# Attention and two expert layers on one core: the wide layer's sums kept in PSUM, and one ring of eight SBUF tiles for its streamed blocks

## The chip, the cores and the metric

The kernel runs on one core of a Trainium2 chip. The metric is device time in microseconds (us) of one execution; a comparison takes the median of several executions. The engines are called as the profile calls them: PE is TensorE's matmul, PEld its weight load, DVE is VectorE, ACT is ScalarE, POOL is GpSimd, and SP issues the DMAs.

## What is computed

```python
def reference(**kwargs):
    ...
    attn_out = _attn_ref(**attn_kwargs)               # (2, 8, 768, 64), masked by hash buckets
    B, H, S, D = attn_out.shape
    x = np.ascontiguousarray(attn_out.transpose(0, 2, 1, 3)).reshape(B * S, H * D)
    x = _moe_ref(x=x, **moe_kwargs)                   # h = max(x @ w_in, 0); (h * h) @ w_out
    return _moe2_ref(x=x, **moe2_kwargs)

def _moe2_ref(x, w_in, w_out, alpha) -> np.ndarray:
    h = x @ w_in                                      # 1536 x 512 by 512 x 2048
    g = np.maximum(h, 0.0) + alpha * np.minimum(h, 0.0)
    return (g @ w_out).astype(np.float32)             # 1536 x 2048 by 2048 x 512
```

There are 1536 tokens, 512 model columns and 2048 hidden columns in both layers. The change touches the second layer only, `_moe2_ref`.

## The kernel before

**Layout of the time.** Attention runs first, then layer one in four chunks of 384 tokens (`feed_forward`), with the rest of attention and the preparation of layer two's weights beside it. Layer two follows in two token halves n = 0 and 1. Each half is a hidden stage, `wide_hidden(n)`, and then a project stage, `whole_project(n)`. The order on the clock of the trace is: hidden 1 (571.2 to 646.2 us), project 1 (to 732.4), hidden 2 (to 811.3), project 2 (last sums at 896, then the output leaves).

**Precision.** Every float32 product is split into a rounded high part and the rest (low), each a float32r tile, and a product takes three matmuls: high by high, high by low, low by high. So every weight or value that PE reads has first gone through an ACT copy (the high part) and a subtract on POOL or DVE (the low part).

**Hidden stage.** The product x @ w_in is done by Strassen and Winograd's scheme: seven products of half-size blocks in place of eight, with sums of blocks before and after. The sums of weights were made earlier and lie in DRAM (`ws`); the sums of x are made by `x_sums`. The stage has 8 iterations f. In each, `w_load(f + 2)` (L888) starts a DMA of 896 KB into `wraw`, a tile of the pool `slots` (3 tiles of 2048 float32 per partition). `w_part(f + 1)` splits it into `wp`: two ACT copies (L895, 128x1024 and 128x768) and two POOL subtracts (L896), into a tile of the pool `parts` (2 tiles). Then 42 matmuls of 128x384 on PE (L873, L874, L875: six for each of the seven products) go into four PSUM banks a, b, c, d in the order 0(a), 4(b), 3(c), 1(a), 5(d), 6(c), 2(d). PSUM has 8 banks for this, so two iterations fit.

Between the products DVE adds blocks (`add`, L879): u2 = b + p1, u4 = c + u2, and the sums h = d + u4, c + u2 and d + u2. p1 is an ACT copy of bank a (L929). Product 1 overwrites a after p1 has read it, product 6 goes on in c after u4 has read it, and product 2 overwrites d after the sum d + u4 has read it. Each of the four results then takes the leaky step, `leaky`: up = Relu(h) on ACT (L910), down = Relu(-h) on ACT (L911), and g = down * (-alpha) + up as a scalar_tensor_tensor on DVE (L912). For quarter 11 the ACT steps read PSUM and write the SBUF tiles `up` and `down`; for the other three, h is the SBUF tile that `add` wrote, and L911 writes over it. So L912 always reads two SBUF tiles. g stays in SBUF for the project stage.

**Project stage.** For each of 16 steps f, `part(f)` brings in one block of w_out by DMA (`wp`, L954, 256 KB), splits it by an ACT copy (L955) and a DVE subtract (L956), and splits the block of g by an ACT copy of 128x768 (`gp`, L959) and a POOL subtract (L960). `wp` and `gp` are each one tile of the pool `slots`. Then 18 matmuls of 128x512 follow, over six banks: 12 with g's high part (L969, L970) and 6 with its low part (L975; in the last step L972, bank by bank). `part(f + 2)` is written after step f. In project 1, `second_x` and `x_sums` for the other half run beside.

**What sets the order.** The Tile scheduler places the instructions of each engine by a priority and by when a tile becomes free; a tile of a pool is handed out once its earlier reader is done. The order on each engine is fixed when the program is built, so a waiting instruction holds all that stand behind it on its engine. SP's DMA queue works in the same way.

Of the kernel before, what the change touches and what calls it, by code (L numbers as in the profile page):

```python
# [7 lines left out]
F32 = mybir.dt.float32  # L8
F32R = mybir.dt.float32r
# [3 lines left out]
AF = mybir.ActivationFunctionType  # L13
ALU = mybir.AluOpType
# [15 lines left out]
def kernel(  # L30
# [20 lines left out]
    nc = tc.nc  # L51
# [3 lines left out]
    P = 128  # L55
    T = S // 2
# [8 lines left out]
    scale = 1.0 / float(D) ** 0.5  # L65

    def pool(name, bufs, stack=ctx, **kw):
        return stack.enter_context(tc.tile_pool(name=name, bufs=bufs, **kw))
# [13 lines left out]
    state = {"attention": True, "moe": False, "s": 0, "m": 0, "h": 0, "whole": state_whole}  # L82
# [35 lines left out]
    def f32(ap):  # L118
        return ap.bitcast(F32)
# [489 lines left out]
    HM = DM // 2  # L609
# [26 lines left out]
    PLACE = (0, 1, 4, 2, 3, 5, 6)  # L636
# [157 lines left out]
    KH = KDM // 2  # L794
# [70 lines left out]
    def slot(name, dt=F32R):  # L865
        return state["slots"].tile([P, 2048], dt, tag="slot", name=name)

    def bank():
        return state["ps"].tile([P, 512], F32, tag="b", name="b")

    def products(ps, w, m, gh, gl, first, last):
        ms = slice(m * P, (m + 1) * P)
        nc.tensor.matmul(ps, w[:, 0, ms], gh, start=first, stop=False, skip_group_check=True)  # L873
        nc.tensor.matmul(ps, w[:, 0, ms], gl, start=False, stop=False, skip_group_check=True)  # L874
        nc.tensor.matmul(ps, w[:, 1, ms], gh, start=False, stop=last, skip_group_check=True)  # L875

    def add(name, ps, x, pool=None):
        t = (pool or state["sums"]).tile([P, T], F32, tag=name, name=name)
        nc.vector.tensor_tensor(t, ps, x, ALU.add)  # L879
        return t  # L880
# [4 lines left out]
    def w_load(f):  # L885
        if f < NF:
            raw_sums[f] = slot("wraw", F32)[:, 0:7 * HM].rearrange("p (a n) -> p a n", n=HM)
            nc.sync.dma_start(out=raw_sums[f], in_=w_sum[f])  # L888

    def w_part(f):  # L890
        if f < NF:
            w = raw_sums.pop(f)
            t = state["parts"].tile([P, 2, 7, HM], F32R, tag="wp", name="wp")
            for i, j in ((0, 4), (4, 7)):
                nc.scalar.activation(t[:, 0, i:j], w[:, i:j], AF.Copy)  # L895
                nc.gpsimd.tensor_tensor(t[:, 1, i:j], w[:, i:j], f32(t[:, 0, i:j]), ALU.subtract)  # L896
            loaded[f] = t

    def wide_hidden(n, between):


        xh, xl = x_parts[n]
        half = [state["g"].tile([P, NF, 2, T], F32, tag=f"g{i}", name=f"g{i}") for i in range(2)]
        quarter = {f"{i + 1}{k + 1}": half[i][:, :, k] for i in range(2) for k in range(2)}
        def leaky(q, h, f):

            col = f + NF * (q[0] == "2")
            up = state["sums"].tile([P, T], F32, tag="up", name="up")
            down = h if q != "11" else state["sums"].tile([P, T], F32, tag="h", name="down")
            nc.scalar.activation(up, h, AF.Relu)  # L910
            nc.scalar.activation(down, h, AF.Relu, scale=-1.0)  # L911
            nc.vector.scalar_tensor_tensor(  # L912
                quarter[q][:, f], down, neg_alpha[:, col:col + 1], up, ALU.mult, ALU.add
            )

        for f in range(NF):
            w_load(f + 2)
            w_part(f + 1)
            w = loaded.pop(f)

            def product(p, ps, first):
                for kk in range(KH):

                    products(ps, w[:, :, PLACE[p]], kk, xh[:, p, kk], xl[:, p, kk], first and kk == 0, kk == KH - 1)

            a, b, c, d = [bank()[:, 0:T] for _ in range(4)]
            product(0, a, True)
            p1 = state["sums"].tile([P, T], F32, tag="p1", name="p1")
            nc.scalar.activation(p1, a, AF.Copy)  # L929
            product(4, b, True)  # L930
            u2 = add("u2", b, p1)
            product(3, c, True)
            u4 = add("u4", c, u2)
            product(1, a, False)
            leaky("11", a, f)
            product(5, d, True)
            leaky("22", add("h", d, u4), f)
            product(6, c, False)
            leaky("12", add("h", c, u2), f)
            product(2, d, False)  # L940
            leaky("21", add("h", d, u2), f)
            between(f)
        return half, quarter

# [85 lines left out]
    state["xraw"] = pool("xraw", 3)  # L1030
    state["xt"] = pool("xt", 2)
    state["xc"] = pool("xc", 1)
    state["slots"] = pool("slot", 3)
    state["parts"] = pool("parts", 2)
    neg_alpha = const.tile([P, KFF], F32, name="neg_alpha")
    nc.vector.tensor_scalar(neg_alpha, alpha_sb[:, 0:KFF], -1.0, None, ALU.mult)
    turned = Background(
# [3 lines left out]
    w_load(0)  # L1041
    w_load(1)
    w_part(0)
    layer1.close()
    state["ps"] = pool("ps2", 8, space=PSUM)
    state["g"] = pool("g", 1, side="right")
    state["sums"] = pool("sums", 2, side="right")
    state["out"] = pool("out", 2, side="right")

    half, quarter = wide_hidden(0, lambda f: None)  # L1050
    steps = second_x(2, bank) + x_sums(1)

# [5 lines left out]
    w_load(0)  # L1058
    w_load(1)
    w_part(0)  # L1060
    half, quarter = wide_hidden(1, lambda f: None)
    whole_project(1, half, lambda f: None)

# [64 lines left out]
```

## Time and profile before

| What | Value |
|---|---|
| Time, three executions | 899.75, 905.48, 909.24 us (median 905.48) |
| The profiled execution | 905.19 us, of which the span is 903.3 us |
| Mean granted clock of TensorE | 0.985 |
| PE busy | 795.3 us (88% of the span) |
| DVE busy | 569.8 us (63%) |
| ACT busy | 510.8 us (57%) |
| POOL busy | 352.6 us (39%) |
| DMA | 143.86 MB, 159 GB/s on average |

The span is the time from the first to the last instruction of the trace; 1.9 us of the execution lie around it. Busy times are those of instructions that do work, and a matmul's own time overlaps with the next one's, so PE's share says little of how much faster it could go. The rows further down are read by stage.

### The profile page before, as it was taken

The page shows a single profiled execution, that of the slowest core. Times are in us where ns is not written, and L with a number is a line of the kernel's source. Part 1 is how long each engine was busy: PE and PEld are TensorE (multiplying, and loading weights), DVE is VectorE, ACT ScalarE, POOL GpSimd, SP SyncE. Part 2 cuts the span into 40 slices and gives each one's busy share as a digit, 9 for nine tenths or more (in the row PEclk, how much of TensorE's full clock was granted, in tenths as well). Part 3 has the DMA queues.
Part 4 walks back from the last instruction along what each step waited for, and adds up shares of the span by engine and source line. Part 5 has one row for each costly group of instructions (what it writes and reads, how often), then busy time and mean ns, then how long its engine had stood idle before and what let it go on. Part 6 is the DMA issues. An engine that isn't in the chain of part 4 may idle for free.

```text
span 903.3 us, 12522 instructions
## 1 busy us (share of the span) xinstructions
PE 795.3 (88%) x4324; PEld 638.1 (71%) x4324; DVE 569.8 (63%) x847; ACT 510.8 (57%) x988; POOL 352.6 (39%) x257
## 2 busy tenths in 40 slices
PE   4899899999999999899999999888978888798885
PEld 2565777777677677677776999777756677786664
DVE  6678799887676577887886352488671138871111
ACT  4677687876565465565656676456542246552222
POOL 1002223334366366433325756235233355423332
PEclk9999899999999999999999999999999999999999
DMA  4957688887867866777566854030011173101112
GB/s 125 227 147 230 202 265 256 250 239 199 247 204 228 204 218 235 249 249 240 190 209 200 290 169 129 15 108 12 24 48 46 51 241 122 54 12 46 48 53 87
DMA packets 56879, 143.86 MB, mean 159 GB/s; under 512 B 7440, under 2 KB 11824, under 8 KB 56816
## 3 DMA queue, kind: packets, MB, share of 16 engines
q1 hardware_dynamic: 56816, 143.07, 51.2%
q8 instruction: 34, 0.56, 0.3%
q14 instruction: 29, 0.24, 0.1%
HBM read 96.82 MB, written 25.48 MB: 135 GB/s over the span
## 4 chain that ended last, share of the span: by engine, by line
PE 20%; DVE 13%; issue 12%; POOL 6%; ACT 6%; DMA 5%; SPq 1%; POOLq 0%; DVEq 0%; ACTq 0%
DVE g L912 4%; POOL gp L960 3%; PE b L969 2%; PE b L970 2%; PE b L975 2%; DMA wf<-w 2%; PE m L424 2%; POOL wp L896 2%; PE b L873 1%; ACT gp L959 1%; DVE u L879 1%; ACT wp L895 1%; PE b L875 1%; PE b L874 1%; PE h L681 1%
## 5 line engine op out<-in xcount | busy, mean ns | idle before, releaser
L644 POOL TENSOR_TENSOR wl<-wf,wh 128x512 fp32r<-128x512 f32 x80 | 111.1, 1391 | 114.0 <-ACT wh L643 86.3
L694 POOL TENSOR_TENSOR gl<-g,gh 128x384 fp32r<-128x384 f32 x64 | 72.9, 1139 | 112.4 <-ACT g L691 53.1
L960 POOL TENSOR_TENSOR gp<-g,gp 128x768 fp32r<-128x768 f32 x32 | 59.4, 1856 | 133.9 <-ACT gp L959 133.9
L643 ACT ACTIVATE wh<-wf 128x512 fp32r<-128x512 f32 x128 | 79.6, 627 | 55.3 <-PE h L682 28.0
L969 PE MATMUL b<-wp,gp 128*128 128x512 f32 x192 | 78.4, 408 | 28.2 <-ACT gp L959 28.2
L393 ACT ACTIVATE sm<-s,low 128x768 f32<-128x768 f32 x84 | 75.5, 898 | 49.1 <-DVE low L390 48.8
L873 PE MATMUL b<-xph,wp 128*128 128x384 f32 x224 | 78.8, 355 | 25.5 <-DVE u L879 23.4
L390 DVE TENSOR_REDUCE low<-s 128x1 f32<-128x768 f32 x84 | 79.9, 952 | 29.7 <-PE s L385 29.0
L896 POOL TENSOR_TENSOR wp<-wraw,wp 128x1024 fp32r<-128x1024 f32 (+1 forms) x32 | 71.7, 2261 | 68.6 <-ACT wp L895 58.2
L956 DVE TENSOR_TENSOR wp<-wp 128x512 fp32r<-128x512 f32 x32 | 22.1, 690 | 114.7 <-ACT wp L955 114.7
L385 PE MATMUL s<-k,q 128*128 128x384 f32 x336 | 81.3, 361 | 13.3 <-ACT sm L393 11.9
L408 PE MATMUL m<-ident,sm 128*128 128x128 f32 x531 | 85.8, 277 | 4.3 <-ACT q L318 1.4
L408 PEld LDWEIGHTS m<-ident,sm 128*128 128x128 f32 x531 | 65.7, 141 | 21.9 <-ACT q L318 2.2
L681 PE MATMUL h<-xh,wh 128*128 128x384 f32 x212 | 78.9, 372 | 2.4 <-ACT xh L452 1.6
L385 PEld LDWEIGHTS s<-k,q 128*128 128x128 f32 x336 | 59.1, 194 | 30.6 <-ACT sm L393 20.4
L875 PE MATMUL b<-xph,wp 128*128 128x384 f32 x224 | 75.4, 344 | 2.2 <-POOL wp L896 2.2
L874 PE MATMUL b<-xpl,wp 128*128 128x384 f32 x224 | 76.9, 343 | 0.0
L912 DVE SCALAR_TENSOR_TENSOR g<-h,neg_alpha,up 128x384 f32<-128x384 f32 x48 | 69.0, 1458 | 11.3 <-ACT h L911 11.3
L970 PE MATMUL b<-wp,gp 128*128 128x512 f32 x192 | 75.3, 392 | 0.0
L683 PE MATMUL h<-xh,wl 128*128 128x384 f32 x212 | 72.5, 342 | 0.8 <-DMA w<-we 0.8
L682 PE MATMUL h<-xl,wh 128*128 128x384 f32 x212 | 72.5, 342 | 0.6 <-POOL xl L453 0.6
L969 PEld LDWEIGHTS b<-wp,gp 128*128 128x128 f32 x192 | 36.0, 188 | 47.2 <-ACT gp L959 40.5
(176 smaller groups left out, 1865.5 us busy)
## 6 DMA issues: line engine op xcount, KB each, us to landing
wf<-w SPq DMA_DIRECT2D x96, 256.0 KB, 2.9
wbits<-in_w_in_dram SPq DMA_DIRECT2D x32, 512.0 KB, 4.8
wbits<-in_w_out_dram SPq DMA_DIRECT2D x32, 512.0 KB, 4.2
wraw<-ws SPq DMA_DIRECT2D x16, 896.0 KB, 4.9
q<-q SPq DMA_DIRECT2D x48, 192.0 KB, 3.0
w<-wf SPq DMA_DIRECT2D x32, 256.0 KB, 2.6
wp<-w SPq DMA_DIRECT2D x32, 256.0 KB, 2.6
k<-kh SPq DMA_DIRECT2D x14, 384.0 KB, 5.9
```

The lines of the kernel that those rows point to most:

```text
L385: nc.tensor.matmul(ps[:, a, 0:HALF], self.q[:, h, i, qs], self.k[:, h, i, ks], start=i == 0, stop=i == 1)
L408: nc.tensor.transpose(ps[:, i * P:(i + 1) * P], pp[:, b * P:(b + 1) * P], ident)
L644: engine.tensor_tensor(lo, w, f32(hi), ALU.subtract)
L681: nc.tensor.matmul(hp, wih[:, ks], xh[:, kk, :], start=first, stop=False)
L873: nc.tensor.matmul(ps, w[:, 0, ms], gh, start=first, stop=False, skip_group_check=True)
L874: nc.tensor.matmul(ps, w[:, 0, ms], gl, start=False, stop=False, skip_group_check=True)
L875: nc.tensor.matmul(ps, w[:, 1, ms], gh, start=False, stop=last, skip_group_check=True)
L896: nc.gpsimd.tensor_tensor(t[:, 1, i:j], w[:, i:j], f32(t[:, 0, i:j]), ALU.subtract)
L912: nc.vector.scalar_tensor_tensor(quarter[q][:, f], down, neg_alpha[:, col:col + 1], up, ALU.mult, ALU.add)
L960: nc.gpsimd.tensor_tensor(t[:, 1], x, f32(t[:, 0]), ALU.subtract)
L969: nc.tensor.matmul(a, g[:, 0, b], w[:, 0], start=f == 0, stop=False)
L970: nc.tensor.matmul(a, g[:, 0, b], w[:, 1], start=False, stop=False)
```

## The change

In `leaky` the second ACT step writes over its input in every case, and in three of four sums of the hidden stage a new helper, `onto`, takes the place of `add`: it writes the sum in PSUM, over the bank that it read, or, for quarter 22, into bank b, which u2 has read by then. So h is always a PSUM bank, L912 reads one PSUM bank and one SBUF tile, and the tiles `h` and `down` are gone. A bank is held until L912 has read it.

The pool `parts` is gone and `slots` grows from 3 tiles to 8. `w_part` takes two of these tiles, one for the high and one for the low part.

```diff
@@ products
-        nc.tensor.matmul(ps, w[:, 0, ms], gh, start=first, stop=False, skip_group_check=True)
+        nc.tensor.matmul(ps, w[0][:, ms], gh, start=first, stop=False, skip_group_check=True)
...
@@ w_part
-            t = state["parts"].tile([P, 2, 7, HM], F32R, tag="wp", name="wp")
+            t = [slot("wp")[:, 0:7 * HM].rearrange("p (a n) -> p a n", n=HM) for _ in range(2)]
             for i, j in ((0, 4), (4, 7)):
-                nc.scalar.activation(t[:, 0, i:j], w[:, i:j], AF.Copy)
-                nc.gpsimd.tensor_tensor(t[:, 1, i:j], w[:, i:j], f32(t[:, 0, i:j]), ALU.subtract)
+                nc.scalar.activation(t[0][:, i:j], w[:, i:j], AF.Copy)
+                nc.gpsimd.tensor_tensor(t[1][:, i:j], w[:, i:j], f32(t[0][:, i:j]), ALU.subtract)
@@ wide_hidden
             up = state["sums"].tile([P, T], F32, tag="up", name="up")
-            down = h if q != "11" else state["sums"].tile([P, T], F32, tag="h", name="down")
             nc.scalar.activation(up, h, AF.Relu)
-            nc.scalar.activation(down, h, AF.Relu, scale=-1.0)
+            nc.scalar.activation(h, h, AF.Relu, scale=-1.0)
             nc.vector.scalar_tensor_tensor(
-                quarter[q][:, f], down, neg_alpha[:, col:col + 1], up, ALU.mult, ALU.add
+                quarter[q][:, f], h, neg_alpha[:, col:col + 1], up, ALU.mult, ALU.add
             )
+
+        def onto(ps, x, to=None):
+
+            to = ps if to is None else to
+            nc.vector.tensor_tensor(to, ps, x, ALU.add)
+            return to
...
-            leaky("22", add("h", d, u4), f)
+            leaky("22", onto(d, u4, b), f)
             product(6, c, False)
-            leaky("12", add("h", c, u2), f)
+            leaky("12", onto(c, u2), f)
             product(2, d, False)
-            leaky("21", add("h", d, u2), f)
+            leaky("21", onto(d, u2), f)
...
-    state["slots"] = pool("slot", 3)
-    state["parts"] = pool("parts", 2)
+    state["slots"] = pool("slot", 8)
```

In the changed kernel the lines behind `leaky` stand 6 further down (`part` is at L960 to L966 there, `onto` adds at L919, and p1 is L935). The scheduler places some instructions anew. First DVE, in the second iteration of hidden 1, from u2 on; the numbers are those of tiles and banks. Before:

```order
L879 TENSOR_TENSOR u2_6710<-b_6693,p1_6702 128x384
L879 TENSOR_TENSOR u4_6718<-b_6694,u2_6710 128x384
L879 TENSOR_TENSOR h_6737<-b_6695,u4_6718 128x384
L912 SCALAR_TENSOR_TENSOR g0_6601<-down_6727,neg_alpha_5790,up_6726 128x384
L879 TENSOR_TENSOR h_6749<-b_6694,u2_6710 128x384
L912 SCALAR_TENSOR_TENSOR g1_6602<-h_6737,neg_alpha_5790,up_6739 128x384
L879 TENSOR_TENSOR h_6761<-b_6695,u2_6710 128x384
L912 SCALAR_TENSOR_TENSOR g0_6601<-h_6749,neg_alpha_5790,up_6751 128x384
L912 SCALAR_TENSOR_TENSOR g1_6602<-h_6761,neg_alpha_5790,up_6763 128x384
```

And DVE in the same iteration of the changed kernel:

```order
L879 TENSOR_TENSOR u2_6706<-b_6689,p1_6698 128x384
L879 TENSOR_TENSOR u4_6714<-b_6690,u2_6706 128x384
L912 SCALAR_TENSOR_TENSOR g0_6599<-b_6688,neg_alpha_5787,up_6722 128x384
L919 TENSOR_TENSOR b_6689<-b_6691,u4_6714 128x384
L919 TENSOR_TENSOR b_6690<-b_6690,u2_6706 128x384
L912 SCALAR_TENSOR_TENSOR g1_6600<-b_6689,neg_alpha_5787,up_6733 128x384
L919 TENSOR_TENSOR b_6691<-b_6691,u2_6706 128x384
L912 SCALAR_TENSOR_TENSOR g0_6599<-b_6690,neg_alpha_5787,up_6744 128x384
L912 SCALAR_TENSOR_TENSOR g1_6600<-b_6691,neg_alpha_5787,up_6755 128x384
```

There are nine instructions in both; the leaky step of quarter 11 now stands ahead of the sum for quarter 22, the sum that product 2 waits for.

The second place is ACT, from the last iterations of hidden 1 to the start of project 1. Before, from the last leaky steps on:

```order
L910 ACTIVATE up_7246<-h_7244 128x384
L911 ACTIVATE h_7244<-h_7244 128x384
L959 ACTIVATE gp_7267<-g0_6601 128x768
L816 ACTIVATE xraw_7297<-b_7323 128x4x128
L816 ACTIVATE xraw_7297<-b_7354 128x4x128
L955 ACTIVATE wp_7288<-wp_7288 128x512
L959 ACTIVATE gp_7292<-g0_6601 128x768
```

And after, in the last iteration and behind it:

```order
L965 ACTIVATE gp_7293<-g0_6599 128x768
L910 ACTIVATE up_7219<-b_7155 128x384
L911 ACTIVATE b_7155<-b_7155 128x384
L832 ACTIVATE xph_7389<-xraw_6563 128x768
L961 ACTIVATE wp_7289<-wp_7289 128x512
L965 ACTIVATE gp_7324<-g0_6599 128x768
L961 ACTIVATE wp_7320<-wp_7320 128x512
L965 ACTIVATE gp_7355<-g0_6599 128x768
```

Before, gp_7267 is the block of step 1, and it stands behind the last leaky step; in the changed kernel gp_7293 is that of step 3, and it stands ahead of it.

The third place is POOL in layer one's last chunk, where wl is the low part of one of layer one's weights, gl that of its hidden values, and wp that of layer two's. Before:

```order
L694 TENSOR_TENSOR gl_5849<-g_5847,gh_5848 128x384
L896 TENSOR_TENSOR wp_6605<-wraw_6573,wp_6605 128x768
L644 TENSOR_TENSOR wl1_5880<-wf_5823,wh1_5879 128x512
L694 TENSOR_TENSOR gl_5899<-g_5897,gh_5898 128x384
L644 TENSOR_TENSOR wl1_5931<-wf_5856,wh1_5930 128x512
L694 TENSOR_TENSOR gl_5950<-g_5948,gh_5949 128x384
L644 TENSOR_TENSOR wl1_5982<-wf_5906,wh1_5981 128x512
L694 TENSOR_TENSOR gl_6007<-g_6005,gh_6006 128x384
```

And after:

```order
L694 TENSOR_TENSOR gl_5896<-g_5894,gh_5895 128x384
L896 TENSOR_TENSOR wp_6604<-wraw_6570,wp_6603 128x1024
L644 TENSOR_TENSOR wl1_5928<-wf_5853,wh1_5927 128x512
L896 TENSOR_TENSOR wp_6604<-wraw_6570,wp_6603 128x768
L694 TENSOR_TENSOR gl_5947<-g_5945,gh_5946 128x384
L644 TENSOR_TENSOR wl1_5979<-wf_5903,wh1_5978 128x512
L896 TENSOR_TENSOR wp_6683<-wraw_6601,wp_6682 128x1024
L896 TENSOR_TENSOR wp_6683<-wraw_6601,wp_6682 128x768
L694 TENSOR_TENSOR gl_6004<-g_6002,gh_6003 128x384
```

In the changed kernel the split of a third block of layer two (wp_6683) has moved up into layer one, between two of its own subtracts; before, it stood behind the last of them.

## Rows read from the trace of the kernel before

**Rows 1.** The page's costliest groups: L912 (busy us, mean ns | idle before, releaser).

```profile
L912 DVE SCALAR_TENSOR_TENSOR g<-h,neg_alpha,up 128x384 f32<-128x384 f32 x48 | 69.0, 1458 | 11.3 <-ACT h L911 11.3
```

**Rows 2.** Windows by stage: us, then busy per engine (instructions), PEclk, DMA share, GB/s.

```profile
500.00:540.00 40.00, 40.00 (x241) 39.81 (x241) 15.44 (x15) 30.15 (x57) 25.30 (x20) 1.00 0.66 228
571.20:646.20 75.00, 62.51 (x337) 59.63 (x338) 59.26 (x71) 42.89 (x84) 28.90 (x13) 0.98 0.14 44
646.20:732.40 86.20, 71.25 (x301) 54.12 (x300) 26.58 (x30) 32.06 (x46) 28.52 (x16) 1.00 0.19 59
732.40:811.30 78.90, 64.80 (x338) 60.97 (x337) 60.20 (x73) 45.67 (x89) 37.19 (x17) 0.96 0.31 103
811.30:893.10 81.80, 67.11 (x277) 50.40 (x276) 11.98 (x18) 23.40 (x33) 27.58 (x15) 1.00 0.16 45
```

**Rows 3.** PE's waits by line, in 571:646, 646:732.4, 732.4:808 and 808:904 (total, times, longest us).

```profile
PE b L873 <- DVE u L879: 12.5, 6, 2.1
...
PE b L969 <- ACT gp L959: 14.2, 14, 2.5
...
PE b L873 <- DVE u L879: 10.9, 6, 2.1
PE b L875 <- POOL wp L896: 2.2, 2, 1.4
...
PE b L969 <- ACT gp L959: 14.0, 15, 0.9
PE b L972 <- POOL gp L960: 0.7, 1, 0.7
```

**Rows 4.** The chain that ended last, 571:735: start us, us, what.

```profile
590.32 1.60 DVE g L912
...
592.70 2.18 DVE g L912
...
677.12 1.37 PE b L975 x6
...
682.43 1.37 PE b L975 x6
```

**Rows 5.** Timeline of hidden stages: start us, us, engine, line, operation.

```profile
588.62 0.33 PE L873 MATMUL b<-xph,wp 128*128 128x384 f32 x1
...
591.22 0.33 PE L873 MATMUL b<-xph,wp 128*128 128x384 f32 x1
...
745.07 4.51 POOL L896 TENSOR_TENSOR wp<-wraw,wp 128x1024 fp32r<-128x1024 f32 x2 [1.29 <-ACT wp L895]
...
745.43 2.46 DVE L912 SCALAR_TENSOR_TENSOR g<-h,neg_alpha,up 128x384 f32<-128x384 f32 x1
...
747.81 0.54 DVE L879 TENSOR_TENSOR u<-b,u 128x384 f32<-128x384 f32 x1
```

**Rows 6.** Durations of single lines, ns min/median/max.

```profile
L912 DVE SCALAR_TENSOR_TENSOR g<-h,neg_alpha,up x48: 607/1164/2507, 578.9 to 813.7; 128x384 f32<-128x384 f32 x48
...
L879 DVE TENSOR_TENSOR h<-b,u x48: 541/558/559, 577.2 to 812.0; 128x384 f32<-128x384 f32 x48
...
L910 ACT ACTIVATE up<-b x16: 472/490/491, 575.7 to 808.1; 128x384 f32<-128x384 f32 x16
...
L895 ACT ACTIVATE wp<-wraw x32: 826/939/1063, 493.3 to 795.0; 128x1024 fp32r<-128x1024 f32 x16, 128x768 fp32r<-128x768 f32 x16
...
L956 DVE TENSOR_TENSOR wp<-wp x32: 679/693/695, 618.8 to 887.8; 128x512 fp32r<-128x512 f32 x32
```

**Rows 7.** Timeline of project 1: one step's end and the next one's start.

```profile
689.14 0.84 ACT L959 ACTIVATE gp<-g 128x768 fp32r<-128x768 f32 x1 [1.90 <-PE b L975]
...
690.04 0.50 PE L969 MATMUL b<-wp,gp 128*128 128x512 f32 x1 [0.93 <-ACT gp L959]
690.06 1.84 POOL L960 TENSOR_TENSOR gp<-g,gp 128x768 fp32r<-128x768 f32 x1 [3.47 <-ACT gp L959]
```

**Rows 8.** Timeline of POOL in layer one's last chunk.

```profile
517.08 1.30 POOL L644 TENSOR_TENSOR wl<-wf,wh 128x512 fp32r<-128x512 f32 x1 [3.07 <-PE m L683]
```

More of the change, by code (lines that the diff above doesn't have):

```diff
@@ L872, in products @@
         ms = slice(m * P, (m + 1) * P)
-        nc.tensor.matmul(ps, w[:, 0, ms], gh, start=first, stop=False, skip_group_check=True)
-        nc.tensor.matmul(ps, w[:, 0, ms], gl, start=False, stop=False, skip_group_check=True)
-        nc.tensor.matmul(ps, w[:, 1, ms], gh, start=False, stop=last, skip_group_check=True)
+        nc.tensor.matmul(ps, w[0][:, ms], gh, start=first, stop=False, skip_group_check=True)
+        nc.tensor.matmul(ps, w[0][:, ms], gl, start=False, stop=False, skip_group_check=True)
+        nc.tensor.matmul(ps, w[1][:, ms], gh, start=False, stop=last, skip_group_check=True)
     def add(name, ps, x, pool=None):
@@ L922, in product @@
                 for kk in range(KH):
-                    products(ps, w[:, :, PLACE[p]], kk, xh[:, p, kk], xl[:, p, kk], first and kk == 0, kk == KH - 1)
+                    products(ps, [x[:, PLACE[p]] for x in w], kk, xh[:, p, kk], xl[:, p, kk], first and kk == 0, kk == KH - 1)
             a, b, c, d = [bank()[:, 0:T] for _ in range(4)]
```

## The prediction

> **What bounds the kernel now.** I read the span stage by stage first [rows 2], then what PE waits for in each stage [rows 3], then the chain that ended last [rows 4], and last the timeline around a wait [rows 5, 7]. Up to 571 us the change touches nothing but POOL's and ACT's order near the end of layer one, where PE is busy without a break (40.00 of 40.00 us in 500 to 540 [rows 2]). Everything else happens in the four stages of layer two, which last 75.0, 86.2, 78.9 and 81.8 us [rows 2] (the last counted to the first finished bank).
>
> How short could they be? In a hidden stage six products' worth of matmuls start 15 instructions apart at 588.62 and 591.22 [rows 5]: 2.60 / 15 = 0.1733 us each. An iteration has 42: 7.28 us, eight take 58.2 us. The stages take 16.8 and 20.7 us more. In a project stage six matmuls take 1.37 us [rows 4], 18 take 4.11 us; the same point of two neighbouring steps lies 682.43 - 677.12 = 5.31 us apart. So 1.20 us of every step is lost.
>
> Who is waited for? In the hidden stages PE waits for DVE's u (12.5 and 10.9 us, in six waits each, up to 2.1 us) and in the project stages for ACT's gp (14.2 and 14.0 us) [rows 3]. DVE's part of this is the leaky step L912. Alone it takes 607 ns, its median is 1164 ns [rows 6], and the 48 of quarters 12, 21 and 22 are busy 69.0 us [rows 1], which is 69.0 - 48 x 0.61 = 39.7 us too many, or 2.5 us an iteration. That is just PE's loss: (75.0 + 78.9) / 16 - 7.28 = 2.34 us. On the chain these are pairs of 1.60 and 2.18 us [rows 4], and the timeline shows what they have in common: while POOL subtracts from 745.07 for 4.51 us, an L912 with two SBUF inputs takes 2.46 us, and an L879 with one input in PSUM takes 0.54 us, in the midst of the same POOL work [rows 5]. So it isn't that DVE is overloaded (59.26 us busy of 75.00); it stands still beside POOL.
>
> In the project stage the loss has another reason: gp of the next step (ACT, 0.84 us from 689.14) starts only when the last matmul of the step before has let its slot go, and PE starts 0.06 us after it ends, having stood for 0.93 us [rows 7]. Three slots hold one and a half steps.
>
> **The change part by part.**
>
> *Leaky step and sums in PSUM.* No instruction is added: four L912, three sums and eight Relu per iteration as before; three sums and four Relu now write PSUM. The rows have no DVE or ACT instruction in this stage that writes PSUM, so that is the unknown price. Reading PSUM is shown: the sum 558 ns, Relu from a bank 490 ns, and 607 ns for the L912 with both inputs in SBUF [rows 6]. Nearest rows for a write are these same steps, so I take 0.49, 0.56 and 0.61 us. The bounds: 0.1 us less each, and three times as much (the blocked L912 of 1.60 us against 0.61 is the dearest thing of that size in the rows).
>
> The rows for a PSUM source show no extra cost beside SBUF (558 against 607 ns). [...]
>
> Does the stage then run at PE's pace? ACT per iteration has p1 and eight Relu at 0.49 and two copies at 0.94 us [rows 6]: 6.3 us. DVE has five sums at 0.56 and four L912 at 0.61: 5.2 us. POOL has two subtracts, 28.90 / 13 x 2 = 4.4 us [rows 2]. All are under 7.28. The order is what is left. Counted from an iteration's first matmul, product 1 can't start before 3.12 us and ends at 4.16; two Relu (to 5.14), the leaky step of quarter 11 that DVE's new order puts ahead (5.75) and the sum for 22 (6.31) follow, and product 2, due at 6.24, waits for that sum. With some 0.05 us from engine to engine this is 0.2 us late: a period of 7.45 us, 59.6 us in all. To that I add 1.5 us, since the blocks of project steps 0 to 3 are now prepared in the last three iterations on ACT, POOL and DVE (before, only step 0 and half of step 1). DVE's L956 among them has two SBUF inputs and can stand behind a POOL subtract of some 2.2 us, ahead of a u. [...] Hidden 1: 62.5 us, a gain of 12.5 (bounds 8 and 16.5).
>
> *Hidden 2* has the same loop, and its start besides: its weights' loads wait for a slot, PE waits 2.2 us for POOL [rows 3]. With eight slots the loads of blocks 0 to 2 stand ahead of the output DMAs on SP, and the split of block 0 ahead of the bank copies on ACT. POOL still needs two subtracts (4.4 us) after project 1's last gp, so I leave 1.2 us of it: 63.7 us, a gain of 15.2 (bounds 10 and 19.5). SP's loads of blocks 3 and 4 now stand between the output's DMAs and wait for POOL; behind them wait banks' copies, not weights, and two banks are spare, so I cost that at nothing; if the cover is gone it is one iteration's wait, 2 us.
>
> *The ring in the project stages.* gp and wp of step f+4 wait for step f's last matmul, so three steps, 12.3 us, cover a chain of DMA, ACT copies, and subtracts of 0.69 and 1.84 us [rows 6, 7]. The 1.20 us goes in 15 steps: 18.0 us; the last step's 0.7 us for POOL [rows 3] goes too. PE is next: 4.11 us a step against ACT's 1.5 and POOL's 1.84. Project 1 gives 18.7 us (to 67.5) and project 2 18.7 us (to 63.1). Lower bound 15 each, if the sums of x for the other half, DVE's and ACT's, still hold up wp now and then in project 1; upper bound 20, PE's 16 x 4.11 = 65.8 us in project 1.
>
> *Layer one's end.* POOL takes two subtracts more, 4.4 us, between its own (the third piece of order), and idles 3.07 us ahead of one step there [rows 8]. What doesn't fit delays gl, and so PE, which has no gap here: 2 us lost (0 to 4). SP's load of block 4 waits for that POOL work, with weights of layer one queued behind; those are fetched two steps early, so nothing.
>
> **Sum.** -12.5 - 18.7 - 15.2 - 18.7 + 2 = -63.1 us. The profiled execution took 905.19 us, close to the median of 905.48, so the forecast is 905.2 - 63.1 = 842 us.
>
> **Rivals.**
>
> *A, both stages at PE's pace.* Nothing in the order costs anything: hidden stages 58.2 and 59.4, projects 65.8 and 62.0, layer one's end 0. The gains are 16.8, 19.5, 20.4 and 19.8, 76.5 in all: 829 us. For it: near the end of layer one PE already runs without a break [rows 2]. Against it: product 2's wait worked out above. Chance 0.10.
>
> *B, leftover waits.* DVE's L956 and the sums of x keep two SBUF inputs and run beside POOL; in before L956 never met POOL (maximum 695 ns [rows 6]), with the ring it can. If each meets a subtract of 1.84 us and this comes out on PE's path in a third of 32 steps, that is 32 / 3 x 1.84 = 20 us; with a third of it covered, 13 us: 855 us. Against it: three steps of lead. Chance 0.12.
>
> *C, the leaky step still stands still beside POOL,* because up, one of its inputs, and g, its output, stay in SBUF. Then only the ring gains: -37.4 in the projects, -3 at hidden 2's start, +2: 867 us. For it: no L912 with one PSUM input is in the trace. Against it: L879 has one SBUF input and an SBUF output too, and runs through at 0.54 us. Chance 0.10.
>
> [...]
>
> *D, slower.* Writing PSUM is dear. The loop of the hidden stage passes four Relu that write PSUM and two sums (22 and 21). At three times their 0.49 and 0.56 us the period is 7.45 + 4 x 0.98 + 2 x 1.12 = 13.6 us against 9.62 now, +64 us in 16 iterations, against -38 from the ring: 931 us. It decides from 0.77 us more per step on (period 12.0). Against it: reads of PSUM show nothing of the kind. Chance 0.03.
>
> *E, the change doesn't do what it says:* slots stay busy because of the scheduler's order, and the banks held longer cost PE what the leaky step gives back. The order speaks against it (blocks of steps 0 to 3 stand ahead of project 1). 905 us, chance 0.02.
>
> **How the numbers follow.** The forecast of 842 us has 0.63, within 833 to 851. Range: down to 830, where A's 829 begins, and up to 862, short of C; left out are C, D, E and a part of A, about 0.19. Three executions of before lie within 1%, so 1%, 9 us, is what can be told from no change. Faster by more: forecast, A, B and C, 0.95. Same: E, 0.02. Slower: D, 0.03.
>
> **What would show it.** Right: all L912 near 0.6 us, none above 1; hidden stages of 62 to 64 us, PE's waits for u under 2 us in each; project steps 4.1 us apart and no wait for gp; a wait of PE for POOL of some 2 us near 510 us. Wrong: L912 still at 1.6 us beside POOL (C); L911 or L919 over 1 us (D); project steps at 4.11 with single gaps behind an L956 of over 1 us (B); steps still at 5.3 us (E).

## The result, and the profile after

The changed kernel takes 843.45 us (median of 4 executions, 841.42 to 846.94) where the kernel before took 907.36 us beside it: a ratio of 0.9314 between the means of the executions, with a 95% interval from 0.9246 to 0.9381. The forecast was 842 us. The profiled execution took 845.0 us with a span of 843.2 us, 60.1 us less than before.

The page of the kernel after, from its top, its list by engine and the chain that ended last:

```profile
span 843.2 us, 12510 instructions
...
PE 784.8 (93%) x4324; PEld 641.8 (76%) x4324; DVE 538.1 (64%) x847; ACT 505.1 (60%) x988; POOL 351.4 (42%) x257
...
PE 23%; DMA 1%; ACT 1%; issue 1%; POOL 0%; DVE 0%; ACTq 0%; POOLq 0%
```

The chain of after can be followed back to 615.69 us. In the 228 us that it covers, PE has 23% of the span of 843.2 us, 194 us, and DVE and POOL have 0% each. The windows of the four stages, hidden 1, project 1, hidden 2 and project 2 (to its first finished bank), and of the start of hidden 2 (columns as in [rows 2]):

```profile
573.40:636.60 63.20, 61.22 (x336) 59.62 (x337) 40.02 (x71) 40.74 (x86) 26.57 (x13) 0.97 0.18 57
636.60:703.36 66.76, 66.76 (x302) 55.30 (x301) 29.20 (x29) 31.10 (x45) 31.51 (x16) 1.00 0.27 81
703.36:770.90 67.54, 62.60 (x338) 60.88 (x337) 41.57 (x74) 43.57 (x89) 33.06 (x17) 0.95 0.34 116
770.90:833.00 62.10, 62.10 (x276) 51.43 (x275) 11.23 (x18) 20.47 (x30) 23.96 (x13) 1.00 0.19 56
703.36:716.00 12.64, 9.56 (x39) 9.24 (x38) 3.77 (x7) 4.92 (x9) 6.47 (x4) 0.73 0.77 267
```

PE is busy for all of 66.76 and all of 62.10 us in the project stages. DVE's 59.26 and 60.20 us in the hidden stages [rows 2] have become 40.02 and 41.57 us with the same instructions. PE's waits by line, in 490:573, 570:635 and 705:770; in the project stages there is none:

```profile
PE acc L712 <- POOL gl L694: 2.2, 2, 1.8
...
PE b L873 <- DVE b L919: 1.9, 1, 1.9
...
PE b L873 <- ACT p L935: 3.1, 1, 3.1
PE b L873 <- DVE b L919: 1.8, 1, 1.8
```

The durations of the lines that answer to [rows 6]:

```profile
L912 DVE SCALAR_TENSOR_TENSOR g<-b,neg_alpha,up x64: 604/617/621, 578.9 to 773.0; 128x384 f32<-128x384 f32 x64
...
L911 ACT ACTIVATE b<-b x64: 479/488/514, 578.4 to 772.5; 128x384 f32<-128x384 f32 x64
...
L919 DVE TENSOR_TENSOR b<-b,u x48: 548/556/567, 579.5 to 771.3; 128x384 f32<-128x384 f32 x48
...
L962 DVE TENSOR_TENSOR wp<-wp x32: 676/692/2328, 616.4 to 823.2; 128x512 fp32r<-128x512 f32 x32
```

No L912 is above 0.621 us, where the longest took 2.507 [rows 6]. The steps that write PSUM cost what they cost with SBUF: 488 ns for Relu(-h) (before, into SBUF, L911 took 485 ns from a bank and 510 from an SBUF tile), 556 ns for the sum (558 [rows 6]). Of these lines only L962, which still has two SBUF inputs, has a long tail. The timeline of two neighbouring iterations of hidden 1, first before, then after:

```profile
589.95 4.51 POOL L896 TENSOR_TENSOR wp<-wraw,wp 128x1024 fp32r<-128x1024 f32 x2 [5.15 <-ACT wp L895]
...
590.32 4.56 DVE L912 SCALAR_TENSOR_TENSOR g<-h,neg_alpha,up 128x384 f32<-128x384 f32 x2 [0.80 <-ACT h L911]
...
599.65 4.50 POOL L896 TENSOR_TENSOR wp<-wraw,wp 128x1024 fp32r<-128x1024 f32 x2 [5.19 <-ACT wp L895]
...
590.25 4.21 POOL L896 TENSOR_TENSOR wp<-wraw,wp 128x1024 fp32r<-128x1024 f32 x2 [3.26 <-ACT wp L895]
590.96 0.62 DVE L912 SCALAR_TENSOR_TENSOR g<-b,neg_alpha,up 128x384 f32<-128x384 f32 x1 [0.91 <-ACT b L911]
...
597.65 4.21 POOL L896 TENSOR_TENSOR wp<-wraw,wp 128x1024 fp32r<-128x1024 f32 x2 [3.19 <-ACT wp L895]
```

L912 at 590.96 lies in the midst of POOL's work and takes 0.62 us. Before, two L912 stand still there one behind the other, for 4.56 us. From POOL work to POOL work it is 597.65 - 590.25 = 7.40 us, where it was 599.65 - 589.95 = 9.70 us before. And in the chain of the project stage, the low matmuls of two neighbouring steps start 643.62 - 639.54 = 4.08 us apart (5.31 before [rows 4]):

```profile
639.54 1.36 PE b L981 x6
...
643.62 1.37 PE b L981 x6
```

One stage is longer than forecast, hidden 2. Two places in the timeline of after show PE's longest waits, the first in hidden 1, the second at the start of hidden 2; the last line is a window, with columns as in [rows 2]:

```profile
615.86 1.84 POOL L966 TENSOR_TENSOR gp<-g,gp 128x768 fp32r<-128x768 f32 x1 [0.96 <-ACT gp L965]
...
616.39 1.87 DVE L962 TENSOR_TENSOR wp<-wp 128x512 fp32r<-128x512 f32 x1 [0.70 <-issue]
...
619.31 0.44 PE L873 MATMUL b<-xph,wp 128*128 128x384 f32 x1 [1.85 <-DVE b L919]
...
707.05 1.79 ACT L895 ACTIVATE wp<-wraw 128x1024 fp32r<-128x1024 f32 x2 [5.29 <-DMA wraw<-ws]
...
708.74 0.58 ACT L989 ACTIVATE y<-b 128x512 f32<-128x512 f32 x1
...
709.22 0.48 ACT L935 ACTIVATE p<-b 128x384 f32<-128x384 f32 x1
...
709.75 0.69 PE L873 MATMUL b<-xph,wp 128*128 128x384 f32 x1 [3.08 <-ACT p L935]
...
708.90:715.70 6.80, 5.95 (x19) 5.95 (x20) 2.99 (x5) 3.06 (x7) 3.48 (x2) 0.50 0.63 198
```

In the first, L962 (the old L956) of a project block stands still beside POOL's gp, and L912 and the sum that PE needs stand behind it on DVE. In the second, p1 of the first iteration stands on ACT behind the copies of weight block 2, which waited 5.29 us for their DMA, and behind a bank copy of the output. PE waits 3.08 us, and from 708.90 to 715.70 the granted clock is 0.50: most of the 5.95 us of matmuls there come behind the wait, and they start 0.32 us apart, where it is 0.17 us at a clock of 1.00. From the first matmul behind the wait to the 19th it is 715.68 - 709.75 = 5.93 us; behind the same wait in the run with three edges (below), at a clock of 1.00, it is 705.00 - 701.77 = 3.23 us. So an estimated 2.7 us of hidden 2 are the clock's and 3.1 us the wait's. In hidden 1, too, the clock stood at 0.50 for 3.4 us from 620.2 us on, behind the wait for L919, which makes an estimated 1.5 us (63.3 us, against 61.8 in the run with 6 output tiles, which has the same wait).

### The profile page after: what moved, and what is told of

Its sections match the earlier page's. It is cut to its first block, busy times and chain, and to the rows that moved or that the text cites. A ratio compares the mean times of both kernels' runs of the same rounds, so it can differ in the third digit from the quotient of the medians.

```text
span 843.2 us, 12510 instructions
## 1 busy us (share of the span) xinstructions
PE 784.8 (93%) x4324; PEld 641.8 (76%) x4324; DVE 538.1 (64%) x847; ACT 505.1 (60%) x988; POOL 351.4 (42%) x257
## 5 line engine op out<-in xcount | busy, mean ns | idle before, releaser
L966 POOL TENSOR_TENSOR gp<-g,gp 128x768 fp32r<-128x768 f32 x32 | 60.5, 1892 | 86.8 <-ACT gp L965 86.7
L896 POOL TENSOR_TENSOR wp<-wraw,wp 128x1024 fp32r<-128x1024 f32 (+1 forms) x32 | 68.2, 2154 | 50.5 <-ACT wp L895 50.5
L385 PEld LDWEIGHTS s<-k,q 128*128 128x128 f32 x336 | 58.8, 193 | 30.0 <-ACT sm L393 19.7
L975 PE MATMUL b<-wp,gp 128*128 128x512 f32 x192 | 75.0, 391 | 0.0
L976 PE MATMUL b<-wp,gp 128*128 128x512 f32 x192 | 74.8, 389 | 0.0
L962 DVE TENSOR_TENSOR wp<-wp 128x512 fp32r<-128x512 f32 x32 | 27.5, 865 | 66.6 <-ACT wp L961 65.1
L644 DVE TENSOR_TENSOR wl<-wf,wh 128x512 fp32r<-128x512 f32 x48 | 41.4, 862 | 44.8 <-ACT wh L643 41.1
L424 PE MATMUL m<-pt,vr 128*64 128x384 f32 x336 | 66.0, 497 | 0.6 <-ACT pt L412 0.6
```

Source lines behind the costliest of these rows:

```text
L385: nc.tensor.matmul(ps[:, a, 0:HALF], self.q[:, h, i, qs], self.k[:, h, i, ks], start=i == 0, stop=i == 1)
L644: engine.tensor_tensor(lo, w, f32(hi), ALU.subtract)
L975: nc.tensor.matmul(a, g[:, 0, b], w[:, 0], start=f == 0, stop=False)
L976: nc.tensor.matmul(a, g[:, 0, b], w[:, 1], start=False, stop=False)
```

## The experiments

All kernels differ from the changed one by the edit shown, and are compared with the kernel before on the same chip in the same hours. The lengths of stages are worked out from the timelines: from the first matmul of a hidden or project stage to the first of the next, and to the end of the last matmul. The first 570 us, which no edit touches apart from their end, vary by 8 us (the first matmul of hidden 1 stands at 568.1 to 576.2 us), so stages tell more than totals where few us matter. A stage is that of one profiled execution, and its clock varies too: hidden 1 of the changed kernel takes 63.3 us at a mean granted clock of 0.97, but 61.8 us in the two runs that don't touch it (split behind p1, 6 output tiles), where the matmuls behind the wait for L919 go on 0.17 us apart. What an edit does to hidden 1 is therefore better measured against 61.8. By the intervals of the totals, only PSUM alone, the ring alone and all edits can be told apart from the changed kernel; what is said of the others rests on their stages.

| Kernel | Median us | Ratio to before (95%) | Hidden 1 | Project 1 | Hidden 2 | Project 2 |
|---|---|---|---|---|---|---|
| before | 907.36 | 1 | 75.1 | 86.2 | 78.9 | 84.7 |
| after | 843.45 | 0.9314 (0.9246 to 0.9381) | 63.3 | 66.5 | 67.6 | 65.3 |
| PSUM alone | 879.66 | 0.9731 (0.9675 to 0.9787) | 64.3 | 86.2 | 65.8 | 84.7 |
| ring alone | 858.13 | 0.9491 (0.9445 to 0.9537) | 70.0 | 66.5 | 74.8 | 65.3 |
| L912 on two SBUF tiles | 850.26 | 0.9386 (0.9338 to 0.9433) | 66.3 | 66.5 | 72.4 | 65.3 |
| sums in SBUF | 843.48 | 0.9314 (0.9272 to 0.9357) | 62.1 | 66.6 | 67.6 | 65.3 |
| split behind p1 | 840.58 | 0.9306 (0.9276 to 0.9336) | 61.8 | 66.6 | 66.2 | 65.3 |
| wp on POOL | 838.86 | 0.9281 (0.9249 to 0.9312) | 60.7 | 66.5 | 66.4 | 65.3 |
| three edges | 834.53 | 0.9232 (0.9203 to 0.9261) | 60.7 | 66.5 | 64.0 | 65.3 |
| 6 slots | 839.54 | 0.9279 (0.9250 to 0.9307) | 62.6 | 68.1 | 65.8 | 65.3 |
| 6 output tiles | 838.85 | 0.9230 (0.9197 to 0.9264) | 61.8 | 66.5 | 63.6 | 65.3 |
| all edits | 833.69 | 0.9177 (0.9141 to 0.9213) | 60.7 | 66.6 | 62.3 | 65.3 |

**The PSUM half alone.**

```diff
-            t = [slot("wp")[:, 0:7 * HM].rearrange("p (a n) -> p a n", n=HM) for _ in range(2)]
+            t = state["parts"].tile([P, 2, 7, HM], F32R, tag="wp", name="wp")
+            t = [t[:, 0], t[:, 1]]
...
-    state["slots"] = pool("slot", 8)
+    state["slots"] = pool("slot", 3)
+    state["parts"] = pool("parts", 2)
```

> The PSUM half of the change alone: slots has 3 tiles and parts 2 again, sums and leaky step stay in PSUM. Theory (L912 stood still beside POOL because it had two SBUF inputs; the project stages lost 1.2 us a step to the depth of the ring; two separate things): every L912 near 0.62 us, hidden 1 near 63 us, project steps 5.31 us apart again, projects 86 and 82 us, total 843.5 + 18 + 19 = 881 us (875 to 887). Rival (the hidden stage was cured by the ring, which lets the weights be split earlier, so that POOL runs at other moments): hidden 1 stays near 75 us and the total near 895 to 905 us.

It took 879.66 us. The hidden stages, 64.3 and 65.8 us, are nearly as short as with the ring, and the project stages are those of before to a tenth. PE's longest waits from 569 to 875 us, over layer two:

```profile
PE b L976 <- ACT gp L966: 28.2, 29, 2.5
PE b L873 <- ACT p L936: 7.2, 6, 1.6
```

So the hidden stage doesn't need the ring for its gain (10.8 and 13.1 us here, without the ring), and the whole gain of the project stages is the ring's.

**The ring alone.**

```diff
-            nc.scalar.activation(h, h, AF.Relu, scale=-1.0)
+            down = h if q != "11" else state["sums"].tile([P, T], F32, tag="h", name="down")
+            nc.scalar.activation(down, h, AF.Relu, scale=-1.0)
...
-            leaky("22", onto(d, u4, b), f)
+            leaky("22", add("h", d, u4), f)
...
```

The other two sums go back to `add` in the same way.

> The ring half alone: 8 slots, no parts, but sums h and down are SBUF tiles as before. Theory: L912 again up to 2.5 us beside POOL, PE waits some 12 us for u in each hidden stage, hidden stages near 75 and 77 us, projects 67 and 62 us, total 843.5 + 12 + 10 = 866 us (860 to 872). Rival (ring cured the hidden stage too): 843 to 850 us.

It took 858.13 us: the leaky step on DVE, L913 in this kernel and the next two, stands still as much as ever (67.1 us for the same 48, 69.0 in [rows 1]), but the hidden stages are only 8.2 us (against 61.8) and 7.2 us longer than with the whole change, not 12 and 10. The total is 2 us below the theory's range and far from the rival's. The timeline of an iteration shows the reason:

```profile
589.82 4.51 POOL L896 TENSOR_TENSOR wp<-wraw,wp 128x1024 fp32r<-128x1024 f32 x2 [4.49 <-ACT wp L895]
590.19 2.45 DVE L913 SCALAR_TENSOR_TENSOR g<-h,neg_alpha,up 128x384 f32<-128x384 f32 x1 [0.55 <-ACT h L912]
592.56 0.54 DVE L879 TENSOR_TENSOR u<-b,p 128x384 f32<-128x384 f32 x1
593.03 1.72 DVE L913 SCALAR_TENSOR_TENSOR g<-h,neg_alpha,up 128x384 f32<-128x384 f32 x1
594.67 0.55 DVE L879 TENSOR_TENSOR u<-b,u 128x384 f32<-128x384 f32 x1
...
595.27 0.44 PE L873 MATMUL b<-xph,wp 128*128 128x384 f32 x1 [1.42 <-DVE u L879]
...
598.81 4.51 POOL L896 TENSOR_TENSOR wp<-wraw,wp 128x1024 fp32r<-128x1024 f32 x2 [4.48 <-ACT wp L895]
```

The scheduler put u2 between the two blocked leaky steps, where before both stood ahead of u2. The iteration is 8.99 us.

**L912 on two SBUF tiles, sums in PSUM; and the mirror image.** The first edit gives Relu(-h) an SBUF tile again, the second makes the three sums SBUF tiles again but has Relu(-h) write the PSUM bank:

```diff
-            nc.scalar.activation(h, h, AF.Relu, scale=-1.0)
+            down = state["sums"].tile([P, T], F32, tag="h", name="down")
+            nc.scalar.activation(down, h, AF.Relu, scale=-1.0)
...
```

> The changed kernel with one edit: Relu(-h) goes to an SBUF tile again, so L912 reads two SBUF tiles; the sums stay in PSUM, the ring stays. Theory (what counts is L912's second SBUF input): as the ring alone, L912 up to 2.5 us, total near 866 us (858 to 872). Rival (what counts is where the sums lie, that is what L919 writes and ACT reads): 843 to 848 us.

```diff
-            leaky("22", onto(d, u4, b), f)
+            leaky("22", add("h", d, u4), f, b)
...
-            leaky("12", onto(c, u2), f)
+            leaky("12", add("h", c, u2), f, c)
...
```

In the mirror image `leaky` takes the bank that Relu(-h) writes as a further argument.

> The mirror image: the three sums are SBUF tiles again, but Relu(-h) goes to the PSUM bank, so L912 reads PSUM and SBUF; the ring stays. Theory: L912 near 0.62 us, total as the changed kernel within 1%, 843 to 850 us (the first Relu of three quarters reads SBUF, 523 instead of 490 ns, some 0.1 us an iteration). Rival (place of the sums counts): near 866 us.

The durations of the leaky step, ns min/median/max, first in the kernel with L912 on two SBUF tiles, then in the mirror image:

```profile
L913 DVE SCALAR_TENSOR_TENSOR g<-down,neg_alpha,up x64: 605/618/2762, 577.4 to 779.2; 128x384 f32<-128x384 f32 x64
...
L913 DVE SCALAR_TENSOR_TENSOR g<-b,neg_alpha,up x64: 604/618/620, 575.2 to 768.2; 128x384 f32<-128x384 f32 x64
```

The mirror image came out as the theory has it: 843.48 us, no leaky step over 620 ns. So one PSUM operand is enough, and where the sums lie makes no difference that shows. The other kernel missed both ranges: 850.26 us, not 866, and above the rival's 848. The leaky step does stand still (64.8 us for 64, up to 2.76 us, against 39.4 in the changed kernel), but the 25 us too many cost only 4.5 us (against 61.8) and 4.8 us in the two stages. Its timeline:

```profile
589.35 4.50 POOL L896 TENSOR_TENSOR wp<-wraw,wp 128x1024 fp32r<-128x1024 f32 x2 [3.64 <-ACT wp L895]
590.07 2.09 DVE L913 SCALAR_TENSOR_TENSOR g<-down,neg_alpha,up 128x384 f32<-128x384 f32 x1 [0.86 <-ACT down L912]
592.09 0.54 DVE L879 TENSOR_TENSOR u<-b,p 128x384 f32<-128x384 f32 x1
592.73 0.56 DVE L879 TENSOR_TENSOR u<-b,u 128x384 f32<-128x384 f32 x1
...
593.34 0.45 PE L873 MATMUL b<-xph,wp 128*128 128x384 f32 x1 [0.34 <-DVE u L879]
...
597.50 4.51 POOL L896 TENSOR_TENSOR wp<-wraw,wp 128x1024 fp32r<-128x1024 f32 x2 [3.65 <-ACT wp L895]
```

Only one blocked leaky step stands ahead of u2 and u4 here; PE waits 0.34 us, and the iteration is 8.15 us. Together with the others this makes a row: two blocked steps ahead of both u's, 9.70 us; two with u2 between them, 8.99; one, 8.15; none, 7.40. What a blocked instruction costs is what stands behind it on DVE. The four kernels differ in more than this order, so the row fits the reading and doesn't prove it.

**What holds hidden 2 up.** First, the ACT copies of weight block 2 are kept behind p1, in hidden 2 alone:

```diff
-            w_part(f + 1)
+            if n == 1 and f == 1:
+                with tc.issue_after(copied.ins):
+                    w_part(f + 1)
+            else:
+                w_part(f + 1)
...
-            nc.scalar.activation(p1, a, AF.Copy)
+            copied = nc.scalar.activation(p1, a, AF.Copy)
```

> The changed kernel with one edge more: in hidden 2 alone, the ACT copies of weight block 2 are kept behind the copy p1 of the first iteration. Theory (hidden 2 is 4 us longer than hidden 1 because those copies stand ahead of p1 on ACT and wait 5.4 us for their DMA, which holds PE 3.1 us and is followed by matmuls at half clock): no wait for p1, hidden 2 at 62 to 64 us, total 843.5 - 4.5 = 839 us (836 to 841). Rival (the block comes too late anyway, since its DMA waits for a slot; PE then waits for POOL's split of it in place of p1): hidden 2 stays at 66 to 68 us, total 842 to 845 us.

The total, 840.58 us, lies in the theory's range, but the stage says otherwise: hidden 2 takes 66.2 us, as the rival had it, though not by its wait for POOL. An estimated 1.5 us of that are the clock's, as in the changed kernel's hidden 1: behind the wait for L919 it is 5.51 us from that L919 (748.12 us) to the next iteration's u2 (753.63), as it is there (5.50 us, 618.71 to 624.21), where the clock stood at 0.50, and not 4.39 us as in this run's own hidden 1 (616.88 to 621.27). The copies do stand behind p1, and p1 still comes late:

```profile
704.99 0.60 ACT L993 ACTIVATE y<-b 128x512 f32<-128x512 f32 x1 [6.56 <-DMA out_dram<-y]
...
705.48 0.48 ACT L939 ACTIVATE p<-b 128x384 f32<-128x384 f32 x1
...
706.02 0.44 PE L873 MATMUL b<-xph,wp 128*128 128x384 f32 x1 [2.68 <-ACT p L939]
```

A bank copy of project 1's output stands ahead of p1. It waits for one of the two tiles y, and so for an output DMA that was issued (698.83 us) behind a weight load of 896 KB (697.99 us). Removing the first lock ahead of p1 had only shown the second. So the pool of y got 6 tiles, as the one edit to the changed kernel:

```diff
-    state["out"] = pool("out", 2, side="right")
+    state["out"] = pool("out", 6, side="right")
```

> The changed kernel with one edit: the pool of output tiles y has 6 tiles in place of 2. The run with the split behind p1 had only moved hidden 2's first wait: p1 of the first iteration still came 2.7 us late, behind a bank copy on ACT that waited 6.6 us for an output DMA to free a y tile. Theory (that copy is the second lock ahead of p1, and the same two tiles stretch the end of the kernel): p1 not waited for or under 1 us, hidden 2 at 62 to 65 us in place of 67.6, the end behind the last matmul 4 to 5 us in place of 7.2, total 843.5 - 6 = 837.5 us (835 to 840). Rival (the output DMAs and weight loads share the queue, so p1's iteration waits for weights or for POOL instead): hidden 2 stays above 66 us, only the end is shorter, total 840 to 842 us.

It took 838.85 us. Hidden 2 fell from 67.6 to 63.6 us, its mean granted clock rose from 0.95 to 1.00, and the end behind the last matmul from 843.2 - 836.2 = 7.0 to 837.3 - 833.4 = 3.9 us. PE's waits in its hidden 2, and ACT's p1 and the copies of weight block 2:

```profile
PE b L873 <- DVE b L919: 3.0, 2, 1.9
PE b L873 <- ACT p L935: 0.3, 1, 0.3
...
705.79 0.49 ACT L935 ACTIVATE p<-b 128x384 f32<-128x384 f32 x1 [0.47 <-PE b L875]
...
708.52 1.80 ACT L895 ACTIVATE wp<-wraw 128x1024 fp32r<-128x1024 f32 x2 [2.23 <-DMA wraw<-ws]
```

The edit did more than free the bank copies: the scheduler now also places the copies of block 2 behind p1, so both locks went at once. The split behind p1 shows that the bank copy alone holds PE for 2.7 us; what the copies of block 2 alone would cost, no run shows. Of what makes up the 4.0 us that the stage gained, the clock's part (an estimated 2.7 us, above) is about as large as that of p1, for which the wait is 2.8 us shorter; a new wait of 1.2 us for L919 stands against both.

**The other wait, L962 beside POOL.**

```diff
-            nc.vector.tensor_tensor(w[:, 1], f32(w[:, 2]), f32(w[:, 0]), ALU.subtract)
+            eng = nc.gpsimd if f < 4 else nc.vector
+            eng.tensor_tensor(w[:, 1], f32(w[:, 2]), f32(w[:, 0]), ALU.subtract)
```

> The changed kernel with the low part of w_out's blocks 0 to 3 subtracted on POOL instead of DVE (POOL then works one after the other, and DVE has no instruction with two SBUF inputs left in the hidden stages). Theory (one wait of 1.9 and one of 1.8 us of PE for L919 come from the DVE subtract that stands still beside POOL's gp): those waits go, hidden 1 at 61 to 62 us, hidden 2 near 65.5 us, total 843.5 - 4 = 839.5 us (837 to 842). Rival (POOL, with 1.3 us more a step, delays gp and the first project steps): 843 to 847 us, with PE waits for POOL at the start of the project stages.

Hidden 1 went from 63.3 to 60.7 us (1.1 us less than the 61.8) and hidden 2 from 67.6 to 66.4; the total is 838.86 us. PE waits 1.5 us for L919 in both stages together (two waits of up to 0.8) where it had waited 3.7, and none for POOL at a project's start.

**Three edges at once,** with the edge on p1 in both halves:

> Both edits above, and the edge on p1 in hidden 1 too, which keeps the split of weight block 2 out of layer one's end (there PE waited some 2 us more for gl). If the three waits are independent: 843.5 - 4.5 - 4 - 2 = 833 us (830 to 837), both hidden stages at 59 to 62 us. If what one edit frees is lost at another place: 837 us or more.

834.53 us: hidden 1 as forecast; hidden 2, at 64.0, still has the wait for the bank copy:

```profile
701.77 0.44 PE L873 MATMUL b<-xph,wp 128*128 128x384 f32 x1 [3.09 <-ACT p L939]
...
701.50:712.00 10.50, 10.23 (x58) 9.97 (x59) 7.11 (x13) 8.61 (x17) 8.10 (x4) 1.00 0.51 156
```

The wait is as long as in the changed kernel, but the clock stays at 1.00 behind it. So the late p1 and the clock are two costs, and the first can come without the second; why the clock fell in one run and not in the other stays open. Over all executions the mean granted clock is 0.983 to 0.989 in the changed kernel and 0.989 to 0.995 here. In layer one's end PE waits 0.6 us for gl at L712, as before the change (2.2 in the changed kernel).

**6 slots in place of 8.**

> The changed kernel with 6 slots in place of 8. Block 2's split then no longer fits ahead of layer one's end or of p1 in hidden 2 by the scheduler's own order. Theory (two steps of lead, 8.2 us, still cover the chain of a project step, about 2.6 us of DMA, 1.5 of ACT and 1.9 of POOL): projects as with 8 slots, no wait for p1, total 838 to 841 us. Rival (the depth of 8 is needed): project steps longer than 4.1 us, total 850 us or more.

839.54 us. Two steps of lead are enough for all but the start: project 1 is 1.6 us longer, of which 1.3 us is one wait for L962. Against that, block 2's split falls out of layer one's end, and hidden 2 is 1.7 us shorter: behind a wait of 3.2 us for L919 its matmuls go on 0.17 us apart, where the changed kernel had its stretch of 0.32. Six are not worse than eight here; which is better can't be told from these totals.

**All edits together.**

> All edits together: split of block 2 behind p1 in both halves, the low part of w_out's blocks 0 to 3 on POOL, 6 output tiles. Theory: 834.5 (the first two) - 3 (hidden 2) - 2.7 (end) = 829 us (826 to 832), both hidden stages at 60 to 61.5 us. Rival (as above): 832 to 835 us.

833.69 us, above the range; the kernel before was at 907.86 us beside it and at 905.0 beside the three edges, so the ratios are the better measure: 0.9177 after 0.9232, which is 5 us. By stage, hidden 2 gained 1.7 and not 3 us, and the end 2.8 us. The windows of its hidden stages:

```profile
573.10:633.80 60.70, 59.90 (x338) 58.28 (x339) 37.21 (x69) 42.54 (x87) 34.61 (x18) 1.00 0.23 75
...
700.30:762.60 62.30, 60.16 (x338) 58.10 (x337) 37.29 (x70) 43.16 (x88) 36.84 (x20) 1.00 0.36 126
```

This kernel beats both: by 8% the one before, and the changed one by 0.9177 / 0.9314, about 1.5%, though these two were compared only by way of the kernel before.

## Why the prediction was right

The sum was -63.1 us, the spans say -60.1. The mechanism was right in its main parts. That the sum came so close is partly luck: the hidden stages gained 4.7 us less than forecast and the projects 2.2 us more. Term by term:

- **Hidden 1,** 75.0 to 62.5: it is 63.3 us. The loop of 7.45 us is 7.40 in the trace. The 1.5 us set aside for the project blocks' preparation is the wait of 1.85 us behind L962, the place that was named. The 1.4 us that 59.6 and 1.5 leave of the 62.5 were the author's estimate for the clock, a term that no run shows by itself; what the trace shows is a clock of 0.50 for 3.4 us, an estimated 1.5 us.
- **Projects,** -18.7 each: project 1 went from 86.2 to 66.5 us (-19.7), project 2 to its first bank copy at 832.8 from 81.8 to 61.9 us (-19.9). The step of 4.11 us is 4.08 and no wait is left; the sums of x, for which the lower bound made room, held nothing up. The gains are nearly rival A's 20.4 and 19.8.
- **Hidden 2,** 78.9 to 63.7: it is 67.6 us, a gain of 11.3 and not 15.2, within the bounds, but outside the 62 to 64 us that were to be a sign of being right. This is the term that was mis-sized. The step that failed was "behind them wait banks' copies, not weights, and two banks are spare, so I cost that at nothing". It looked at SP and at the banks, and not at the order on ACT: ahead of p1 stand there the copies of weight block 2, whose load went out at 701.55 us only, and a bank copy, and p1 is on PE's path. In place of the 1.2 us left for POOL, PE waits 3.1 us for p1, and the clock costs an estimated 2.7 us where the same 1.4 were counted. Even the same sentence's "2 us" for the case that the cover is gone was below the wait. The run with 6 output tiles, without this wait and at a clock of 1.00, takes 63.6 us, 0.1 from the forecast.
- **Layer one's end,** +2: PE's wait for gl at L712 grew from 0.6 to 2.2 us, +1.6, and goes back to 0.6 with the edge on p1. Hidden 1 starts 2.3 us later in this trace, but that lies within the variation of the first 570 us.
- **"That is just PE's loss"** (2.5 us too many in L912 an iteration, 2.34 lost by PE) held for the old order on DVE alone. With the ring alone the leaky step has 2.4 us too many, and the iteration is 8.99 - 7.40 = 1.6 us longer.

**The cause, L912's second SBUF input,** is shown by the mirror image and the PSUM half alone. It also decided against rival C, whose price was off: it gave the ring alone 3 us in the hidden stages (867 us in all), and that kernel takes 858; DVE's order changed with the ring, as its timeline shows. In the rows, L912 with one SBUF input runs at 0.62 us in the midst of POOL's subtracts, with two it takes up to 2.76 us, and L962, left with two, up to 2.33 us.

**The price of PSUM,** the unknown, is nothing that shows: writes at 488 ns (Relu) and 556 ns (sum), so rival D falls. Reading it shows no price either: minimum and median of L912 are 604 and 617 ns with one PSUM input, and 605 and 618 ns in the run with L912 on two SBUF tiles.

**Rival A** (829 us, all at PE's pace) is nearly the kernel with all edits, 833.69: what kept the changed kernel from it were the waits of PE that the runs took away one by one, and the clock behind two of them. (Some 2.4 us of that kernel's gain are the shorter end, which A hasn't.) **Rival B's** mechanism was there, but ahead of the project stages, in two places, of 1.85 and 1.83 us, and not in ten. Two more L962, of 2.32 and 2.33 us in project 1, cost PE nothing. **E** didn't happen.

## What to carry to other kernels

Where an engine is "busy" for far longer than its instructions take alone, look for what runs on its neighbour at that moment: here one operand moved to PSUM took 10.8 and 13.1 us out of two stages (the run with PSUM alone) without one instruction less. How much a blocked instruction costs is read from the order behind it, not from its own duration (here 9.70, 8.99 and 8.15 us an iteration, against 7.40). And when a first wait is removed, list everything that stands ahead of the late instruction on its engine, output copies too: here p1 had two locks ahead of it, and with the first removed the second still held PE for 2.7 us.

## What the runs showed that was not expected

The same blocked leaky step cost between 2.3 us and 0.75 us an iteration, by the number of such steps that the scheduler had put ahead of two additions (9.70, 8.99 and 8.15 against 7.40 us). An output DMA, which gives its tile back some 2.2 us after its issue at the kernel's end, took 6.1 us to land behind a weight load of 896 KB at the start of hidden 2; there, two tiles of output were too few. And the same wait of 3.1 us for p1 was followed by a clock of 0.50 in one kernel (67.6 us for hidden 2) and of 1.00 in another (64.0), so part of what looked like the price of the wait was the clock's.
